# Weight chunks, a held load and a new written order in a linear-attention and FFN kernel

## The chip, the core and the metric

The kernel runs on one core of a Trainium2 chip. The core has a matrix engine (TensorE, PE in the profile), three engines for elementwise work (VectorE or DVE, ScalarE or ACT, GpSimd or POOL), and SyncE (SP), which here only issues DMAs. Each engine has its own instruction queue and works through it in order; between engines, semaphores make one wait for another. Matrix products read SBUF, the on-chip memory, and write PSUM, a small accumulator memory divided into banks. Data moves between the chip's main memory and SBUF by 16 DMA engines that all queues share.

The metric is the device time of one execution in microseconds (us).

## What is computed

Two stages run one after the other. The first is a causal linear attention with decay over 4 batches, 8 heads, 768 positions and a head size of 64; each head has its own decay `lam`. The second is an FFN on the 3072 resulting rows of 512, with a sine in its activation:

```python
intra = np.einsum('bhic,bhjc->bhij', qb, kb) * Dmask[None]
intra = np.einsum('bhij,bhjd->bhid', intra, vb)
inter = np.einsum('bhid,bhde->bhie', qb * lam_pow[None], kv_state)
out[:, :, sl] = intra + inter
kv_state = lam_block * kv_state + np.einsum('bhsd,bhse->bhde', kb_dec, vb)
# then, with x the attention's rows
h = x @ w_in                      # 512 -> 2048
s = np.sin(alpha * h)
g = h + s * s / (alpha + 1e-09)
return g @ w_out                  # 2048 -> 512
```

Inputs and output are float32; the kernel works in bfloat16 and accumulates in float32.

## The kernel before

The work is cut into six groups of 512 rows, and each group's attention into four units, numbered u = 0 to 23 (group u // 4). A unit is 256 positions of one batch and four heads.

A unit takes these steps. Three loads on SP's queue bring q, k and v in float32, 256 KB each (`ld.u.0`, `ld.u.1`, `ld.u.2`; line 256, tiles st_q, st_k, st_v, eight buffers of each). `sq`, `sk` (line 297) multiply q and k by powers of the decay and give bfloat16 tiles QL and KD; `cv` casts v. QL and KD are transposed into QT: units 0 to 7 do that on TensorE (`tq`, `tk`, line 324, then the copies `tcq`, `tck` out of PSUM), units 8 to 23 by DMA transposes on SP's queue (`tdq`, `tdk`, line 342). `s` makes scores (line 365), `m` masks them on VectorE (line 375), `k` makes the unit's state (line 401), `kc` copies it, `a` and `n` decay and accumulate it (lines 427, 431, 439). `oi` and `o` (lines 452, 466) make the output, and `x` copies it into xt, the FFN's input.

For each group g, FFN1 has 16 steps `f1.g.f` of four 128x128 by 512 products (line 489), one for each 128 columns of w_in. The first four are cut in two halves (`f1a.g.f`, then `f1.g.f`), so that the first half can start when the group's units 0 and 1 are done. `sin` (line 509), `sqr` (line 516 or 518) and `stt` (line 523) make the activation into gall. FFN2 has steps `f2.g.m.j` (line 532): 128 rows m, and a quarter j of the 2048 columns, of four products each. Step j needs activations 4j to 4j+3 and the w_out chunk j. `oc` copies the result, `st` stores it on SP's queue. The last 128 rows are done in two halves (`lt`, `ltc`, lines 555 and 565), whose last store ScalarE issues.

The weights come by DMAs that GpSimd issues and that cast float32 to bfloat16: `wi` for w_in (line 266), here five DMAs of 2, 2, 4, 4 and 4 times 128 columns (256 KB or 512 KB in SBUF), and `wo` for w_out (line 273), four of 512 KB, chunk j for FFN2's quarter j. The first of them waits until `loads[GATE]` has landed, v of unit 2. Everything behind it in GpSimd's queue waits with it.

Nothing is scheduled by a program at run time or at build time: the string ORDER lists every step with its engine (T, V, A, G, S for TensorE, VectorE, ScalarE, GpSimd, SyncE) and, for products, the PSUM bank. Reading it from start to end gives each engine's queue. `ld.4.0`, the first load of group 1 (the second group), has a wait added by hand: it is issued only after the FFN1 step named in HOLD, and all that SP issues later stands behind it. `w.n` puts n products of zeros into TensorE's queue (line 595), which nothing reads; 28 more run at the start (line 569).

Of the kernel before, what the change touches and what calls it, by code (L numbers as in the profile page):

```python
# [18 lines left out]
ld.0.0:S tab:V ld.0.1:S ld.0.2:S cv.0:A sq.0:V sk.0:G w.4:T:s1 tq.0:T:5 tcq.0:V w.5:T:s1 tk.0:T:5  # L19
tck.0:V k.0:T:0,1 a.0.0:V ld.1.0:S w.3:T:s0 s.0:T sq.1:G oi.0:T tq.1:T:2 kc.0.0:A kc.0.1:A tcq.1:A  # L20
n.0.0:G ld.1.1:S sk.1:V m.0.0:V ld.1.2:S cv.1:G tk.1:T:1 tck.1:A w.4:T:h0 k.1:T:0,2 m.0.1:V o.0:T
kc.1.0:A kc.1.1:A x.0.0:A s.1:T a.1.0:V m.1.0:V ld.2.0:S ld.2.1:S ld.2.2:S sq.2:G sk.2:G tq.2:T:1
w.3:T:okv oi.1:T tk.2:T:2 m.1.1:V o.1:T tcq.2:A cv.2:A tck.2:A x.1.0:A k.2:T:0,1 ld.3.0:S ld.3.1:S
ld.3.2:S sq.3:V sk.3:V wi.0:G wi.1:G wi.2:G cv.3:G kc.2.0:A x.1.1:A s.2:T m.2.0:V w.2:T:h3 tq.3:T:3
m.2.1:V tcq.3:A kc.2.1:A a.2.0:V tk.3:T:2 tck.3:A w.6:T:h3 k.3:T:3,1 wi.3:G n.1.0:G a.3.0:V s.3:T
oi.2:T o.2:T m.3.0:V x.2.0:A x.2.1:A kc.3.0:A m.3.1:V kc.3.1:V f1a.0.0:T:2 f1a.0.1:T:0 ap:T al:V
oi.3:T o.3:T f1a.0.2:T:1 f1a.0.3:T:3 x.3.0:V x.3.1:A f1.0.0:T f1.0.1:T sin.0.0:A sin.0.1:A sqr.0.0:V
sqr.0.1:V stt.0.0:V wi.4:G wo.0:G a.1.1:G n.2.0:G n.1.1:G f1.0.2:T f1.0.3:T f1.0.4:T:5 f1.0.5:T:4
sin.0.2:A stt.0.1:V sin.0.3:A sin.0.4:A sqr.0.2:G sqr.0.3:A w.3:T:h0 f1.0.6:T:0 sin.0.5:A sin.0.6:A
stt.0.2:V stt.0.3:V f1.0.7:T:2 sqr.0.4:G sqr.0.5:A sqr.0.6:A a.2.1:G stt.0.4:V n.3.0:G wo.1:G  # L30
sin.0.7:A stt.0.5:V sqr.0.7:V stt.0.6:V stt.0.7:V f1.0.8:T:3 f1.0.9:T:5 sin.0.8:A sqr.0.8:G
f1.0.10:T:4 sin.0.9:A sqr.0.9:V sin.0.10:A sqr.0.10:G ld.4.0:S ld.4.1:S ld.4.2:S ld.5.0:S ld.5.1:S
ld.5.2:S ld.6.0:S ld.6.1:S ld.6.2:S ld.7.0:S ld.7.1:S ld.7.2:S ld.8.0:S f1.0.11:T:1 stt.0.8:V
stt.0.9:V sin.0.11:A wo.2:G sq.4:G wo.3:G cv.4:G sqr.0.11:V stt.0.10:V sk.4:G stt.0.11:V f1.0.12:T:0
w.3:T:h3 f1.0.13:T:3 sin.0.12:A sin.0.13:A sqr.0.12:A sqr.0.13:V stt.0.12:V stt.0.13:V f1.0.14:T:2
sq.5:G a.3.1:G a.0.1:G n.0.1:G sk.5:G cv.5:G n.3.1:G sq.6:G sk.6:G cv.6:G sq.7:G sk.7:G f1.0.15:T:4
sin.0.14:A sin.0.15:A sqr.0.14:A sqr.0.15:A stt.0.14:V stt.0.15:V f2.0.1.0:T:1 f2.0.1.1:T
f2.0.0.0:T:3 tq.4:T:2 f2.0.0.1:T tcq.4:A k.4:T:4,5 kc.4.0:A kc.4.1:A a.4.0:V tk.4:T:2 tck.4:A
f2.0.2.0:T:0 oi.4:T tq.5:T:2 s.4:T f2.0.2.1:T m.4.0:V m.4.1:V tcq.5:A f2.0.0.2:T f2.0.2.2:T tk.5:T:2
f2.0.1.2:T tck.5:V s.5:T f2.0.0.3:T m.5.0:V oc.0.0:A f2.0.1.3:T oc.0.1:V o.4:T x.4.0:A k.5:T:2,3  # L40
kc.5.0:A a.5.0:V m.5.1:V kc.5.1:A f2.0.2.3:T tq.6:T:1 oi.5:T tk.6:T:2 o.5:T oc.0.2:A k.6:T:3,0
tck.6:V kc.6.0:V tcq.6:A n.4.0:G cv.7:G s.6:T m.6.0:V f2.0.3.0:T:1 m.6.1:V tq.7:T:2 tcq.7:A ld.8.1:S
# [84 lines left out]
def kernel(  # L127
# [14 lines left out]
    B, H, S, D = q.shape  # L142
# [10 lines left out]
    GATE = (2, 2)  # L153
    HOLD = (0, 9)
# [478 lines left out]
```

## Time and profile before

Seven runs took 222.51 to 225.04 us, with a median of 224.04. The profiled execution took 222.52 us, of which its records span 220.7 us.

| What | Value |
|---|---|
| median of 7 runs | 224.04 us |
| profiled execution | 222.52 us |
| its span | 220.7 us |
| TensorE's granted clock in it, mean | 0.996 |
| first product of FFN1 (`f1a.0.0`) | 18.36 us |
| load `ld.4.0` issued | 30.19 us |
| last product ends | 216.8 us |

The page gives busy time by engine, the chain of waits (from the last instruction back to whatever released each step), groups of instructions by line, and DMA issues. The timeline gives instructions in order of time, equal neighbours merged; a bracket at a line's end is idle time of that engine just before it, and what ended it. "PE" lines are products, "SPq" and "POOL ... DMA_DIRECT2D" lines are issues of DMAs: their time is that of the issue, not of the transfer. Where a DMA's landing is given, it is the time of its semaphore.

### The profile page before, as it was taken

How to read it: one execution, taken by the hardware profiler on the slowest of the kernel's cores; microseconds unless marked ns; L12 is line 12 of the kernel's file. 1: busy time of each engine (PE TensorE's matmuls, PEld its weight loads, DVE VectorE, ACT ScalarE, POOL GpSimd, SP SyncE). 2: the span in 40 equal slices, each digit the busy share in tenths (PEclk: the TensorE clock that was granted, in tenths of full speed). 3: DMA queues.
4: the chain of work that ended last, by engine and by line, in shares of the span. 5: the costliest groups of instructions: out<-in, count | busy, mean ns of one | idle time of the engine just before them, and what ended most of it. 6: DMA issues, size and time to landing. Idle time of an engine off the chain costs nothing.

```text
span 220.7 us, 5409 instructions
## 1 busy us (share of the span) xinstructions
PE 210.2 (95%) x2110; PEld 108.5 (49%) x2110; DVE 127.9 (58%) x218; ACT 126.4 (57%) x232; POOL 138.7 (63%) x208
## 2 busy tenths in 40 slices
PE   8789799999999999899999999999999999999992
PEld 6557344556755534345545444445444444444462
DVE  3694779348599988328477655357564537333020
ACT  3283696335599999254676489425873755544101
POOL 6597476869989889999969758586260703031000
PEclk9999999999999999999999999999999999999998
DMA  5999999999996899999796993325205202020824
GB/s 137 297 189 148 206 161 258 237 298 292 215 184 160 221 197 267 286 212 217 144 242 167 262 137 72 74 71 146 48 0 119 50 1 48 0 50 0 180 61 93
DMA packets 64377, 33.92 MB, mean 154 GB/s; under 512 B 19664, under 2 KB 61408, under 8 KB 64352
## 3 DMA queue, kind: packets, MB, share of 16 engines
q1 hardware_dynamic: 59488, 29.31, 58.4%
q0 software_dynamic: 4752, 4.19, 12.4%
q8 instruction: 16, 0.26, 0.5%
q10 hardware_dynamic: 112, 0.07, 0.1%
q14 instruction: 9, 0.07, 0.1%
HBM read 27.28 MB, written 6.29 MB: 152 GB/s over the span
## 4 chain that ended last, share of the span: by engine, by line
PE 73%; DMA 12%; POOL 10%; issue 1%; DVE 1%; SPq 0%; ACT 0%; POOLq 0%; ACTq 0%
PE ops L532 36%; PE hps L489 27%; DMA w_in_sb<-in_moe_w_in_dram 4%; PE okv L466 2%; DMA QT<-KD 2%; PE sp L365 2%; DMA st_k<-in_k_dram 2%; DMA st_v<-in_v_dram 2%; PE ops L555 2%; POOL s L518 1%; PE okv L452 1%; POOL kvbd L431 1%; POOL KD L297 1%; POOL QL L297 1%; DMA lam_bc<-in_lam_dram 1%
## 5 line engine op out<-in xcount | busy, mean ns | idle before, releaser
L489 PE MATMUL hps<-xt,w_in_sb 128*128 128x512 bf16 (+1 forms) x416 | 91.5, 363 | 1.8 <-DMA w_in_sb<-in_moe_w_in_dram 1.4
L523 DVE SCALAR_TENSOR_TENSOR gall<-s,r_sb,hps 128x512 bf16<-128x512 bf16 x96 | 68.6, 744 | 36.6 <-ACT s L516 22.6
L532 PE MATMUL ops<-w_out_sb,gall 128*128 128x512 bf16 x368 | 86.6, 379 | 0.0
L509 ACT ACTIVATE s<-hps,alpha_sb 128x512 bf16<-128x512 f32 x96 | 63.9, 685 | 37.2 <-PE hps L489 35.2
L518 POOL TENSOR_TENSOR s<-s 128x512 bf16<-128x512 bf16 x30 | 31.1, 1042 | 47.9 <-ACT s L509 46.3
L489 PEld LDWEIGHTS <-w_in_sb 128*128 128x128 bf16 x416 | 38.4, 98 | 40.5 <-DMA w_in_sb<-in_moe_w_in_dram 1.7
L532 PEld LDWEIGHTS <-gall 128*128 128x128 bf16 x368 | 34.3, 98 | 38.5
L516 ACT ACTIVATE s<-s 128x512 bf16<-128x512 bf16 x58 | 35.3, 627 | 1.3 <-DVE gall L523 0.5
L375 DVE TENSOR_TENSOR ST<-sp,mask 128x512 bf16<-128x512 f32 x48 | 31.8, 684 | 5.9 <-PE sp L365 5.7
L279 ACT COPY ob<-ops 128x512 f32<-128x512 f32 (+1 forms) x15 | 8.3, 555 | 30.6 <-PE ops L532 18.3
L297 POOL TENSOR_TENSOR QL<-st_q,E 128x512 bf16<-128x512 f32 x22 | 22.9, 1043 | 3.1 <-DMA st_q<-in_q_dram 2.9
L297 POOL TENSOR_TENSOR KD<-st_k,R 128x512 bf16<-128x512 f32 x22 | 23.0, 1044 | 1.9 <-DMA st_k<-in_k_dram 1.1
L431 POOL TENSOR_TENSOR kvbd<-kvx,LBD 128x256 bf16<-128x256 f32 x32 | 19.6, 614 | 2.5
L281 DVE COPY ob<-ops 128x512 f32<-128x512 f32 x10 | 6.9, 688 | 17.2 <-PE ops L532 17.2
L427 POOL TENSOR_TENSOR kvx<-kva,kvs 128x128 f32<-128x128 f32 x32 | 14.8, 462 | 1.6 <-DVE kva L281 1.6
L279 ACT CAST xt<-okv 128x512 bf16<-128x512 f32 (+1 forms) x17 | 8.8, 525 | 5.2 <-PE okv L466 3.8
L281 POOL CAST VB<-st_v 128x512 bf16<-128x512 f32 x15 | 9.2, 613 | 3.3 <-DMA st_v<-in_v_dram 3.3
L281 DVE CAST xt<-okv 128x512 bf16<-128x512 f32 (+1 forms) x10 | 6.6, 664 | 7.9 <-PE okv L466 7.7
L365 PE MATMUL sp<-QT 64*64 64x128 bf16 x384 | 9.9, 220 | 1.3 <-DMA QT<-KD 1.1
L466 PE MATMUL okv<-ST,VB 64*64 64x128 bf16 x384 | 10.2, 221 | 0.0
L439 POOL TENSOR_TENSOR kvs<-kvx,LHP 128x128 f32<-128x128 f32 x24 | 9.5, 401 | 0.0
L365 PEld LDWEIGHTS <-QT 64*64 64x64 bf16 x384 | 6.6, 106 | 5.0 <-issue 1.7
(60 smaller groups left out, 120.3 us busy)
## 6 DMA issues: line engine op xcount, KB each, us to landing
st_q<-in_q_dram SPq DMA_DIRECT2D x24, 256.0 KB, 4.7
st_k<-in_k_dram SPq DMA_DIRECT2D x24, 256.0 KB, 4.6
st_v<-in_v_dram SPq DMA_DIRECT2D x24, 256.0 KB, 4.8
out_dram<-ob SPq DMA_DIRECT2D x46, 128.0 KB, 2.5
w_out_sb<-in_moe_w_out_dram POOLq DMA_DIRECT2D x4, 512.0 KB, 8.7
w_in_sb<-in_moe_w_in_dram POOLq DMA_DIRECT2D x3, 512.0 KB, 10.7
w_in_sb<-in_moe_w_in_dram POOLq DMA_DIRECT2D x2, 256.0 KB, 4.7
QT<-QL SPq DMA_TRANSPOSE x16, 3.7
```

What stands on the lines that cost most here:

```text
L279: nc.scalar.copy(out=out, in_=in_)
L281: eng.tensor_copy(out=out, in_=in_)
L297: eng.tensor_tensor(out=t[:], in0=stage[u, j][:].rearrange("p h two e -> p two h e"), in1=tab[:, :, hh * HH:(hh + 1) * HH].unsqueeze(3).to ...
L365: nc.tensor.matmul(out=sp[hd][half[c], par, hp, :], lhsT=QT[half[hd], 1, par, hp, half[c]], rhs=QT[half[hd], 0, :, hp, half[c]], start=Tru ...
L375: nc.vector.tensor_tensor(out=stm[u][:, hd], in0=sps[u][hd][:], in1=mask[:].unsqueeze(2).to_broadcast([P, 2, 2, P]), op=ALU.mult)
L431: eng.tensor_tensor(out=kvbd[u, c][:], in0=x.unsqueeze(2).to_broadcast([P, 2, 2, D]), in1=LBD[:, 2 * hh:2 * hh + 2, :].unsqueeze(3).to_bro ...
L489: f1mm[g, f] = nc.tensor.matmul(out=hps[g, f][:].rearrange("p (b i) -> p b i", b=2)[:, bs] .rearrange("p b i -> p (b i)"), lhsT=w_in_sb[:, ...
L509: nc.scalar.activation(out=s1[g, f][:], in_=hps[g, f][:], func=ACTF.Sin, scale=alpha_sb[:, f:f + 1])
L516: nc.scalar.activation(out=s2[g, f][:], in_=x[:], func=ACTF.Square)
L518: eng.tensor_tensor(out=s2[g, f][:], in0=x[:], in1=x[:], op=ALU.mult)
L523: nc.vector.scalar_tensor_tensor(out=gall[g][:, f, :], in0=s2.pop((g, f))[:], scalar=r_sb[:, f:f + 1], in1=hps.pop((g, f))[:], op0=ALU.mul ...
L532: nc.tensor.matmul(out=ops[g, m][:], lhsT=gall[g][:, f, m * P:(m + 1) * P], rhs=w_out_sb[:, f, :], start=(f == 0), stop=(f == NFC - 1))
```

## The change

Three constants change. w_in comes in four DMAs of 4 x 128 columns instead of five. The first of these waits for k of unit 2 instead of v of unit 2. `ld.4.0` waits for FFN1 step 14 of group 0 instead of step 9. The string ORDER is replaced as a whole. It has the same steps with these differences in number: one `wi` less; 20 instead of 33 warm-up products between the steps; some copies, casts, scalings and squares on another engine (ScalarE has 10 steps more, VectorE 9 fewer, GpSimd 2 fewer). No function changes. The lists below are cut to the first stage and the end; in both the middle is left out.

```diff
--- before.py
+++ after.py
@@ -16,111 +16,111 @@
 ORDER = """
-ld.0.0:S tab:V ld.0.1:S ld.0.2:S cv.0:A sq.0:V sk.0:G w.4:T:s1 tq.0:T:5 tcq.0:V w.5:T:s1 tk.0:T:5
...
-ld.3.2:S sq.3:V sk.3:V wi.0:G wi.1:G wi.2:G cv.3:G kc.2.0:A x.1.1:A s.2:T m.2.0:V w.2:T:h3 tq.3:T:3
-m.2.1:V tcq.3:A kc.2.1:A a.2.0:V tk.3:T:2 tck.3:A w.6:T:h3 k.3:T:3,1 wi.3:G n.1.0:G a.3.0:V s.3:T
...
-sqr.0.1:V stt.0.0:V wi.4:G wo.0:G a.1.1:G n.2.0:G n.1.1:G f1.0.2:T f1.0.3:T f1.0.4:T:5 f1.0.5:T:4
-sin.0.2:A stt.0.1:V sin.0.3:A sin.0.4:A sqr.0.2:G sqr.0.3:A w.3:T:h0 f1.0.6:T:0 sin.0.5:A sin.0.6:A
-stt.0.2:V stt.0.3:V f1.0.7:T:2 sqr.0.4:G sqr.0.5:A sqr.0.6:A a.2.1:G stt.0.4:V n.3.0:G wo.1:G
...
-f1.0.10:T:4 sin.0.9:A sqr.0.9:V sin.0.10:A sqr.0.10:G ld.4.0:S ld.4.1:S ld.4.2:S ld.5.0:S ld.5.1:S
-ld.5.2:S ld.6.0:S ld.6.1:S ld.6.2:S ld.7.0:S ld.7.1:S ld.7.2:S ld.8.0:S f1.0.11:T:1 stt.0.8:V
-stt.0.9:V sin.0.11:A wo.2:G sq.4:G wo.3:G cv.4:G sqr.0.11:V stt.0.10:V sk.4:G stt.0.11:V f1.0.12:T:0
-w.3:T:h3 f1.0.13:T:3 sin.0.12:A sin.0.13:A sqr.0.12:A sqr.0.13:V stt.0.12:V stt.0.13:V f1.0.14:T:2
-sq.5:G a.3.1:G a.0.1:G n.0.1:G sk.5:G cv.5:G n.3.1:G sq.6:G sk.6:G cv.6:G sq.7:G sk.7:G f1.0.15:T:4
-sin.0.14:A sin.0.15:A sqr.0.14:A sqr.0.15:A stt.0.14:V stt.0.15:V f2.0.1.0:T:1 f2.0.1.1:T
-f2.0.0.0:T:3 tq.4:T:2 f2.0.0.1:T tcq.4:A k.4:T:4,5 kc.4.0:A kc.4.1:A a.4.0:V tk.4:T:2 tck.4:A
-f2.0.2.0:T:0 oi.4:T tq.5:T:2 s.4:T f2.0.2.1:T m.4.0:V m.4.1:V tcq.5:A f2.0.0.2:T f2.0.2.2:T tk.5:T:2
-f2.0.1.2:T tck.5:V s.5:T f2.0.0.3:T m.5.0:V oc.0.0:A f2.0.1.3:T oc.0.1:V o.4:T x.4.0:A k.5:T:2,3
-kc.5.0:A a.5.0:V m.5.1:V kc.5.1:A f2.0.2.3:T tq.6:T:1 oi.5:T tk.6:T:2 o.5:T oc.0.2:A k.6:T:3,0
...
-st.4.2.0:S st.4.2.1:S f2.5.0.3:T f2.5.1.0:T:5 f2.5.1.1:T f2.5.1.2:T f2.5.1.3:T f2.5.2.0:T:3
-f2.5.2.1:T f2.5.2.2:T f2.5.2.3:T lt.0:T:2 lt.1:T:4 st.4.0.0:S st.4.0.1:S oc.5.0:A st.5.0.0:S
-st.5.0.1:S oc.5.1:V st.5.1.0:S st.5.1.1:S oc.5.2:V st.5.2.0:S st.5.2.1:S ltc.0:A ltc.1:A
+ld.0.0:S ld.0.1:S ld.0.2:S ld.1.0:S tab:V sq.0:V ld.1.1:S ld.1.2:S sk.0:G w.4:T:h2 tq.0:T:2 cv.0:A
+tk.0:T:4 k.0:T:0,1 a.0.0:V sk.1:V ld.2.0:S tcq.0:A tck.0:A w.4:T:s0 s.0:T sq.1:G kc.0.0:A oi.0:T
+tq.1:T:2 tcq.1:A ld.2.1:S ld.2.2:S ld.3.0:S ld.3.1:S wi.0:G ld.3.2:S wi.1:G tk.1:T:0 tck.1:A cv.1:A
...
+kc.2.1:A x.1.1:A w.3:T:okv oi.2:T cv.3:G o.2:T x.2.0:A x.2.1:A k.3:T:2,3 kc.3.0:A kc.3.1:A m.3.0:V
+m.3.1:V n.0.0:G wi.2:G wi.3:G wo.0:G wo.1:G a.0.1:G a.3.0:V ap:T f1a.0.0:T:1 f1a.0.1:T:5 oi.3:T
+o.3:T al:V f1a.0.2:T:0 f1a.0.3:T:4 x.3.0:V x.3.1:A f1.0.0:T sin.0.0:A sqr.0.0:V f1.0.1:T sin.0.1:A
+n.0.1:G sqr.0.1:G stt.0.0:V f1.0.2:T n.2.0:G stt.0.1:V wo.2:G a.2.1:G f1.0.3:T sin.0.2:A sin.0.3:A
...
+stt.0.5:V stt.0.6:V stt.0.7:V f1.0.8:T:5 sin.0.8:A f1.0.9:T:4 sin.0.9:A sqr.0.8:G sqr.0.9:G
+stt.0.8:V stt.0.9:V f1.0.10:T:3 sin.0.10:A sqr.0.10:A stt.0.10:V f1.0.11:T:1 f2.0.0.0:T:2
+f1.0.12:T:0 sin.0.11:A sin.0.12:A sqr.0.11:V sqr.0.12:A f1.0.13:T:5 f1.0.14:T:3 sin.0.13:A
+stt.0.11:V f2.0.0.1:T f2.0.1.0:T:1 f1.0.15:T:4 f2.0.1.1:T f2.0.1.2:T f2.0.0.2:T ld.4.0:S stt.0.12:V
+ld.4.1:S ld.4.2:S ld.5.0:S ld.5.1:S ld.5.2:S ld.6.0:S ld.6.1:S ld.6.2:S ld.7.0:S ld.7.1:S ld.7.2:S
+ld.8.0:S ld.8.1:S ld.8.2:S sin.0.14:A sqr.0.13:A ld.9.0:S ld.9.1:S ld.9.2:S stt.0.13:V wo.3:G
+n.3.0:G a.3.1:G n.3.1:G sin.0.15:A f2.0.2.0:T:0 n.1.0:G a.1.1:G sqr.0.14:G n.1.1:G stt.0.14:V
+sqr.0.15:G sq.4:G sk.4:G stt.0.15:V f2.0.0.3:T sq.5:G sk.5:G oc.0.0:A cv.4:A sq.6:G sk.6:G
+f2.0.2.1:T f2.0.1.3:T tq.4:T:5 tk.4:T:3 f2.0.2.2:T tcq.4:V tck.4:V s.4:T k.4:T:2,3 kc.4.0:A kc.4.1:A
+cv.5:A oc.0.1:V m.4.0:V a.4.0:V f2.0.2.3:T tq.5:T:4 tk.5:T:3 oi.4:T k.5:T:1,2 m.4.1:V oc.0.2:A o.4:T
+cv.6:G tcq.5:A kc.5.0:A tck.5:V s.5:T tq.6:T:0 n.4.0:G x.4.0:A sq.7:G sk.7:G kc.5.1:V a.5.0:V
+tk.6:T:3 f2.0.3.0:T:2 m.5.0:V m.5.1:V tcq.6:A oi.5:T a.4.1:G sq.8:G sk.8:G tck.6:A ld.10.0:S
+ld.10.1:S ld.10.2:S k.6:T:1,0 kc.6.0:A kc.6.1:A cv.7:A o.5:T a.6.0:V x.5.0:A s.6:T m.6.0:V m.6.1:V
...
+f2.5.1.1:T f2.5.1.2:T f2.5.1.3:T f2.5.2.0:T:2 f2.5.2.1:T f2.5.2.2:T oc.5.0:A st.5.0.0:S st.5.0.1:S
+oc.5.1:A st.5.1.0:S st.5.1.1:S f2.5.2.3:T lt.0:T:0 oc.5.2:A ltc.0:A lt.1:T:1 st.5.2.0:S ltc.1:A
+st.5.2.1:S
 """
...
@@ -150,8 +150,8 @@
     NFC = DFF // P
     NU = 4 * NG
     RING = 8
-    GATE = (2, 2)
-    HOLD = (0, 9)
+    GATE = (2, 1)
+    HOLD = (0, 14)
     XSPLIT = (1, 2, 3)
     N0 = 28
     assert NDC == HP
@@ -233,7 +233,7 @@
     w_out_sb = wpool.tile([P, NFC, DM], BF16, name="w_out_sb")
 
     WCH = 4
-    W_IN = (2, 2, 4, 4, 4)
+    W_IN = (4, 4, 4, 4)
     BANK = ("h0", "h1", "h2", "h3", "s0", "s1")
 
     def psum(shape, dtype, name, bank):

```

In the new order `wi.0` and `wi.1` stand behind `sq.1` in GpSimd's queue, `wi.2`, `wi.3`, `wo.0` and `wo.1` follow `n.0.0`, `wo.2` follows `n.2.0`, and `wo.3` follows `sqr.0.9`. On TensorE ten steps of FFN2 of group 0 stand ahead of `tq.4`, where there were three.

## The prediction

> **What bounds the kernel now.** I read the page's busy row first, then the chain of waits, then the timeline of TensorE for every place where it waits.
>
> ```profile
> PE 210.2 (95%) x2110; PEld 108.5 (49%) x2110; DVE 127.9 (58%) x218; ACT 126.4 (57%) x232; POOL 138.7 (63%) x208
> PE 73%; DMA 12%; POOL 10%; issue 1%; DVE 1%; SPq 0%; ACT 0%; POOLq 0%; ACTq 0%
> 14.87 9.35 DMA w_in_sb<-in_moe_w_in_dram
> 24.27 1.90 PE hps L489 x8
> 26.55 6.20 PE hps L489 x28
> 32.79 0.50 PE bz L595 x3
> 33.34 2.75 PE hps L489 x12
> ```
>
> TensorE is busy in 210 of 220.7 us, so the end is set by when it starts real work and by what it waits for after that. The chain shows the start: the third w_in DMA, issued at 14.87, lands at 24.22 and releases the FFN1 step f1.0.4 at 24.27. From there the chain is almost all TensorE. The timeline gives its waits in brackets:
>
> ```profile
> 24.27 1.90 PE L489 MATMUL hps<-xt,w_in_sb 128*128 128x512 bf16 x8 [1.41 <-DMA w_in_sb<-in_moe_w_in_dram]
> 81.66 1.02 PE L489 MATMUL hps<-xt,w_in_sb 128*128 128x512 bf16 x4 [0.32 <-DVE gall L523]
> 89.75 0.42 PE L365 MATMUL sp<-QT 64*64 64x128 bf16 x16 [1.08 <-DMA QT<-KD]
> ```
>
> These are the only bracketed waits from 18.4 us on: 1.41 + 0.32 + 1.08 = 2.81 us. The rest is matmuls, so the change can win from three things only: those waits, TensorE work that is not needed, and an earlier start.
>
> **TensorE work.** The products are the same in both orders. Two things differ. After f1a.0.0 the old order has two warm-up groups of three (26.00 and 32.79; 0.55 us each until the next product), the new one has one: **-0.55**. The other ten fewer warm-ups lie before f1a.0.0, where TensorE waits anyway: nothing. Then the alternation between the 64-row attention products (k, s, o) and all others:
>
> ```profile
> 38.73 1.03 PE L532 MATMUL ops<-w_out_sb,gall 128*128 128x512 bf16 x4
> 39.69 0.32 PE L401 MATMUL kvp<-VB,KD 64*64 64x64 bf16 x16
> ...
> 53.17 0.42 PE L365 MATMUL sp<-QT 64*64 64x128 bf16 x16
> 53.42 0.29 PE L401 MATMUL kvp<-VB,KD 64*64 64x64 bf16 x16
> ```
>
> Start to start, four FFN2 matmuls take 0.96 us ahead of a 64-row block (38.73 to 39.69), but 0.86 ahead of a 128-row one (40.18 to 41.04). A block of scores takes 0.25 us ahead of another 64-row block (53.17 to 53.42), but 0.35 ahead of FFN2 (45.60 to 45.95). So going down and back costs 0.20 us. Counted in the order after f1a.0.0, the old list goes down 42 times, the new 38: 4 x 0.20 = **-0.80**.
>
> **The front: w_in.** The two old 256 KB chunks land at 17.15 and 19.57, 2.42 apart; the last 512 KB chunks at 26.82 and 29.34, 2.5 apart. A small chunk costs the queue as much as a large one (the trace has 512 packets for either), so four instead of five frees some 2.4 us. The gate moves from st_v to st_k of unit 2 (landings 12.44 and 11.54), and wi.0 stands behind sq.1 on POOL (done 9.09) instead of sk.2 (done 13.22): the issue moves from 13.17 to about 11.6. POOL waits there for the gate, with wi.1, sq.3, cv.2 and cv.3 behind it; unit 3's q lands only at 13.34, so the POOL work behind loses nothing.
>
> When data flows is not certain. In the old trace wi.0's first packet comes 1.6 us after its issue; wo.2's comes 3.7 us after (32.93 to 36.6), while loads filled the engines. So flow starts between 13.2 and 15.3. Here a rule speaks against the change. The Trainium skill, DMA: Bandwidth & Descriptors, "Queues, rings and completion order", says that each DMA engine takes turns between queues, packet by packet. The row nearest to that is st_k landing beside w_out: 5.8/9.5/11.0 us (minimum, median, maximum) in 30 to 42 us, against 4.1/5.4/5.7 alone at the start. By the rule, from 13.2 on the remaining two loads (about 660 packets, ending at 14.4 alone) would end near 18; unit 3's mask work on VectorE would come late and f1a.0.0 move from 18.3 to 19.9. By the 3.7 us row nothing collides, and only the early gate is wasted. Between the two I take the flow from about 14.5.
>
> Now FFN1. Following the new order by the durations of the old rows (mask 0.64 twice per unit, scale 0.69 on VectorE or 1.04 on POOL, copies 0.59 on ScalarE), with the loads landing as before: the second mask of unit 1 ends at 13.9, unit 2's at 16.35, s.3 comes at 16.4, oi.2 at 17.25, k.3 at 17.9, and f1a.0.0 at **18.3**, as before (18.36). Chunk 0 needs 2.4 us (row of the first chunk) to 4.65 us (19.57 to 24.22, the third) of flow: landed between 15.6 and 19.9. Chunk 1, which now holds f1.0.4, comes 2.6 later: 18.2 to 22.5. So the 1.41 us wait before f1.0.4 goes, if chunk 0 is there by 18.3; if it lands at 19.9, the wait has only moved ahead of f1a.0.0. Gain 0 to 1.41, and -0.2 by the collision; I take **-0.90**.
>
> A second rule speaks against it: TensorE: Matmul & The Clock Gate, Part 1, says that after an idle window of about 3.4 us the clock halves. PEclk is 1.00 across the old wait of 1.41 us. The longest new wait I find is 1.6 us (chunk 0 at 19.9). By the row this costs nothing; by the rule a wait beyond 3.4 us would make the next 3.4 us half as fast, +1.7. I take the row.
>
> **The hold.** SP's queue stops at ld.4.0 until f1.0.14 instead of f1.0.9; behind it stand every later load, all DMA transposes and all stores. With f1.0.4 near 23.4 and 0.863 us per FFN1 or FFN2 step (four matmuls), f1.0.14 is done near 34.3, against 30.19 before. The work that hides this: f2 steps are moved ahead of unit 4's transposes, ten instead of three, so TensorE reaches tq.4 near 42.9. The loads then run alone, where before they shared the engines:
>
> ```profile
> 28.55 0.79 POOL L273 DMA_DIRECT2D w_out_sb<-in_moe_w_out_dram  x1
> 32.93 0.80 POOL L273 DMA_DIRECT2D w_out_sb<-in_moe_w_out_dram  x1
> 36.66 0.79 POOL L273 DMA_DIRECT2D w_out_sb<-in_moe_w_out_dram  x1
> 36.44 2.39 SPq L256 DMA_DIRECT2D st_k<-in_k_dram  x1
> 38.87 3.25 SPq L256 DMA_DIRECT2D st_v<-in_v_dram  x1
> 42.16 1.25 SPq L256 DMA_DIRECT2D st_q<-in_q_dram  x1
> ```
>
> At 36 to 44 us one load issue takes 1.3 to 3.3 us, because w_out is in the engines. In the new order wo.0 and wo.1 are issued right behind wi.3 (near 18), wo.2 behind sqr.0.1 (near 24), wo.3 behind sqr.0.9 (near 30.5). At 2.5 us a chunk the queue ends with wo.3 near 36 to 38. f2.0.0.3, the first user, comes near 40.3: 2 us to spare. ld.4.0 lands near 38.5, then 0.9 us each: unit 7 near 48.5, against 49.2 to 51.4 before. POOL scales unit 4 after sqr.0.15 (38.8): ready at 40.8, 2 us ahead of tq.4. After tq.4 only 6 f2 steps are left as filler, where the old order had 13. VectorE has there 8 masks (5.1), 4 kvbd (1.7), 4 copies of transposes (1.7) and one each of kva, ob and xt (1.6), 10.1 us within TensorE's 12. Followed unit by unit it is never more than 0.3 us late. I count the hold at 0.
>
> **What was late next.** The waits at 81.66 and 89.75 came from VectorE and from SP's queue (a transpose issued at 84.83, landing 4.87 us later). SP should reach ld.10.0 some 3 us earlier. Adding up the orders by the rows' durations from f1a.0.0 on, POOL has 42 us of work ahead of sk.13 instead of 47, TensorE 69 ahead of s.13 instead of 66. So both waits should go: **-1.40**. But ScalarE gets 4 us more work and no order meets its own plan exactly: I put half of that back, **+0.70**.
>
> **The end.** st.5.2.1 now stands behind the last piece's DMA on SP. Before, the last copy is followed by a DMA of 2.22 us (issued by ScalarE). Now 0.51 us of SP's issue come first, then about 2.3 us: 0.51 + 2.3 - 2.2 = **+0.64**, rounded up.
>
> **Sum**: -0.55 - 0.80 - 0.90 - 1.40 + 0.70 + 0.64 = -2.3 us. The profiled execution took 222.52 (220.7 and 1.8 around it), so 220.2; the runs' median is 224.04, 1.5 above it, so 224.04 - 2.3 = **221.7**.
>
> **Rivals.** (a) *No change*, 223.7 (chance 0.18): the collision eats the front (-0.90 becomes +0.2), and the two later waits are replaced by equal ones (+0.70). -2.3 + 1.1 + 0.7 = -0.5. For it: ScalarE and POOL are busy 5.3 of 5.5 us between 60 and 72. Against: POOL and SP run ahead.
> (b) *Slower*, 225.4 (0.28): the last w_out chunk becomes the wait. f2.0.0.3 used to start at 45.95, just after wo.3 had landed at 45.71, 9.05 us after its issue; now TensorE stands at it near 40.3 with unit 4 queued behind. At 44.0 it waits 3.7: -2.3 + 3.7 = +1.4. It costs the whole gain from a landing at 42.6, and decides for slower from 43.7. For it: wo.2 took 3.7 us to start and 8.44 to land beside loads. Against: it is issued 6 us earlier, ahead of the loads.
> (c) *Nothing hidden is exposed and w_in comes early*: all of 1.41 and nothing put back, -3.5, 220.5. This is the forecast's lower part.
> Forecast with (c): 0.54.
>
> About 0.5% (1.1 us) can be told from no change. Faster 0.54, same 0.18, slower 0.28. The range goes from 219.5 (-3.5 and 1 us for how runs scatter) to 226.0, which takes in (a) and (b); the forecast's own is 219.5 to 222.9.
>
> **What would show it.** f1.0.4 starts near 23.4 with no wait above 0.5; no wait for w_out at f2.0.0.3; tq.4 near 43; no bracket above 0.5 at s.12 to s.16; four fewer descents on TensorE; the last store issued by SP after the last copy. Wrong if f1a.0.0 starts after 19.9, if wo.3 lands after 42, or if new brackets past 60 us add up to more than 2 us.

## The result and the profile after

Twelve runs of the changed kernel have a median of 221.16 us (219.55 to 224.77); the kernel before, on the same chip, took 223.75 us. The ratio is 0.9874, with an interval of 0.9841 to 0.9906: faster by 2.1 to 3.6 us. Ratios and intervals here are of the fast runs alone (those at most 1.5% above the fastest of the same kernel), so they are not the quotients of the medians. On two more chips the unaltered changed kernel gave 221.52 us (0.9917, 0.9887 to 0.9946) and 221.28 us (0.9912, 0.9878 to 0.9946). By the medians the gain is 1.9 to 2.6 us; the prediction was 2.3 (224.0 to 221.7).

Three profiles of the changed kernel exist, and they differ: their runs took 224.77, 222.39 and 219.92 us. The first one is of the longest of its twelve runs. Its busy row, its granted clock in 40 slices, and its chain of waits by engine:

```profile
PE 210.4 (94%) x2097; PEld 109.2 (49%) x2097; DVE 123.5 (55%) x209; ACT 130.5 (59%) x242; POOL 139.1 (62%) x206
PEclk9999999999999999969999999999999999999999
PE 71%; POOL 9%; DMA 8%; SPq 4%; issue 3%; ACT 2%; DVE 1%; POOLq 0%; ACTq 0%
```

TensorE is still the bound, but one slice of the clock row, the 18th, is a 6. The timeline of TensorE, first at the start of FFN1 and then at that slice:

```profile
17.89 0.49 PE L595 MATMUL bz<-zeros 128*128 128x256 bf16 x3 [0.83 <-ACT xt L279]
...
19.27 1.05 PE L489 MATMUL hps<-xt,w_in_sb 128*128 128x256 bf16 x8
...
21.00 4.30 PE L489 MATMUL hps<-xt,w_in_sb 128*128 128x256 bf16 x31
...
93.83 0.42 PE L466 MATMUL okv<-ST,VB 64*64 64x128 bf16 x16
96.03 0.42 PE L365 MATMUL sp<-QT 64*64 64x128 bf16 x16 [1.78 <-DMA QT<-KD]
96.38 3.25 PE L489 MATMUL hps<-xt,w_in_sb 128*128 128x512 bf16 x8
```

The wait of 1.41 us for w_in is gone: from 21.00 on, FFN1 runs through f1.0.4 (at 23.63) without a bracket. f1a.0.0 itself comes at 19.27, 0.9 later than before, held by ScalarE's copy of xt. The two later waits of before are gone too, but a new one of 1.78 us stands at 96.03, at s.14, for its DMA transpose (`tdk.14`, the transpose of k for unit 14); two smaller ones, of 0.36 and 0.18, stand at 73.19 and 77.58. After s.14, eight products of FFN1 take 3.25 us; at full speed they take 1.9 (24.27 in the profile before). The granted clock and the busy time of the engines in three neighbouring stretches of 3.41 us show why:

```profile
93.35:96.76 3.41, 1.63 (x37) 0.78 (x36) 0.27 (x1) 1.33 (x3) 3.25 (x8) 1.00 0.95 146
96.76:100.17 3.41, 3.41 (x10) 1.22 (x8) 3.02 (x5) 1.81 (x3) 3.33 (x6) 0.50 0.54 114
100.18:103.59 3.41, 3.41 (x46) 1.61 (x45) 1.39 (x3) 1.18 (x3) 1.54 (x3) 1.00 0.58 134
```

The columns are the stretch, its length, the busy time of PE, PEld, DVE, ACT and POOL, then the granted clock, the DMA share and GB/s. In the first stretch TensorE is busy for 1.63 us; in the next its clock is 0.50; then it is 1.00 again. So this run lost 1.78 us by the wait and some 1.7 by the clock.

The second profile waits 0.60 us at 67.07 and 1.15 at s.14, and its clock stays full. The third, the control on the last chip, has no such wait: span 218.1 us, and no bracket above 0.16 us from 18 us on. In the table, f1a.0.0 and f1.0.4 are steps of FFN1, f2.0.0.3 the first step that needs the last w_out chunk, tq.4 the first transpose of group 1.

| start of | before | after, first | second | third |
|---|---|---|---|---|
| f1a.0.0 | 18.36 | 19.27 | 19.00 | 18.84 |
| f1.0.4 | 24.27 | 23.63 | 23.36 | 23.20 |
| f2.0.0.3 | 45.95 | 40.75 | 40.48 | 40.33 |
| tq.4 | 38.51 | 43.34 | 43.07 | 42.91 |
| s.14 (its place in the order differs) | 99.02 | 96.03 | 95.34 | 92.85 |
| wait at s.14 | none | 1.78 | 1.15 | none |
| end of the last product | 216.81 | 218.12 | 215.75 | 213.23 |
| span | 220.74 | 222.99 | 220.61 | 218.10 |
| span less the last product's end | 3.93 | 4.87 | 4.87 | 4.87 |

### The profile page after: what moved, and what is told of

Read it like the earlier page. It is cut to its first block, busy times and chain, and to the rows that moved or that the text cites. A ratio compares the mean times of both kernels' runs of the same rounds, so it can differ in the third digit from the quotient of the medians.

```text
span 223.0 us, 5364 instructions
## 1 busy us (share of the span) xinstructions
PE 210.4 (94%) x2097; PEld 109.2 (49%) x2097; DVE 123.5 (55%) x209; ACT 130.5 (59%) x242; POOL 139.1 (62%) x206
## 4 chain that ended last, share of the span: by engine, by line
PE 71%; POOL 9%; DMA 8%; SPq 4%; issue 3%; ACT 2%; DVE 1%; POOLq 0%; ACTq 0%
PE ops L532 33%; PE hps L489 28%; DMA st_k<-in_k_dram 3%; DMA QT<-KD 3%; SPq L256 2%; PE okv L466 2%; POOL QL L297 2%; DMA st_v<-in_v_dram 2%; PE sp L365 2%; POOL KD L297 2%; PE ops L555 2%; PE okv L452 1%; POOL kvbd L431 1%; POOL kvs L439 1%; SPq L342 1%
## 5 line engine op out<-in xcount | busy, mean ns | idle before, releaser
L518 POOL TENSOR_TENSOR s<-s 128x512 bf16<-128x512 bf16 x34 | 35.1, 1043 | 43.8 <-ACT s L509 38.5
L489 PEld LDWEIGHTS <-w_in_sb 128*128 128x128 bf16 x416 | 39.1, 98 | 40.3 <-issue 2.4
L516 ACT ACTIVATE s<-s 128x512 bf16<-128x512 bf16 x54 | 33.3, 630 | 0.7
L297 POOL TENSOR_TENSOR KD<-st_k,R 128x512 bf16<-128x512 f32 x21 | 21.8, 1044 | 2.6 <-PE sp L365 2.0
L279 ACT COPY ob<-ops 128x512 f32<-128x512 f32 (+1 forms) x16 | 8.9, 558 | 23.1 <-PE ops L532 17.6
L279 ACT CAST xt<-okv 128x512 bf16<-128x512 f32 (+1 forms) x21 | 11.4, 546 | 10.3 <-PE okv L466 8.8
L427 POOL TENSOR_TENSOR kvx<-kva,kvs 128x128 f32<-128x128 f32 x32 | 14.7, 458 | 3.7 <-ACT kva L279 1.9
L279 ACT CAST VB<-st_v 128x512 bf16<-128x512 f32 x13 | 8.1, 619 | 3.5 <-DMA st_v<-in_v_dram 3.5
L452 PEld LDWEIGHTS <-kvbd 128*128 128x128 bf16 x80 | 6.1, 98 | 5.1 <-DVE kvbd L431 0.6
L452 PE MATMUL okv<-QT,kvbd 128*128 128x128 bf16 x80 | 8.4, 219 | 0.2
```

Of the source, the lines that this page charges most:

```text
L279: nc.scalar.copy(out=out, in_=in_)
L297: eng.tensor_tensor(out=t[:], in0=stage[u, j][:].rearrange("p h two e -> p two h e"), in1=tab[:, :, hh * HH:(hh + 1) * HH].unsqueeze(3).to ...
L452: nc.tensor.matmul(out=okv[u][:, c, hp * P:(hp + 1) * P], lhsT=sts[c][:, hp].rearrange("p two e -> p (two e)"), rhs=QT[:, 0, :, hp, half[c ...
L489: f1mm[g, f] = nc.tensor.matmul(out=hps[g, f][:].rearrange("p (b i) -> p b i", b=2)[:, bs] .rearrange("p b i -> p (b i)"), lhsT=w_in_sb[:, ...
L516: nc.scalar.activation(out=s2[g, f][:], in_=x[:], func=ACTF.Square)
L518: eng.tensor_tensor(out=s2[g, f][:], in0=x[:], in1=x[:], op=ALU.mult)
```

## The experiments

Each kernel ran against the kernel before on the same chip (median 223.4, 223.9 and 223.46 us on the three).

| kernel | median, us | ratio to before (interval) |
|---|---|---|
| **first chip** | | |
| after_again: the changed kernel | 221.52 | 0.9917 (0.9887 to 0.9946) |
| tail_swap | 220.73 | 0.9882 (0.9844 to 0.9919) |
| hold9 | 220.40 | 0.9888 (0.9844 to 0.9931) |
| five_chunks | 221.89 | 0.9923 (0.9892 to 0.9955) |
| **second chip** | | |
| before_4chunks | 222.81 | 0.9947 (0.9914 to 0.9980) |
| sp14 | 222.58 | 0.9947 (0.9907 to 0.9987) |
| order_only | 223.29 | 0.9974 (0.9934 to 1.0014) |
| warm6 | 224.44 | 1.0034 (0.9995 to 1.0074) |
| **third chip** | | |
| after_third: the changed kernel | 221.28 | 0.9912 (0.9878 to 0.9946) |
| tail_hold11 | 220.60 | 0.9869 (0.9827 to 0.9910) |
| order_warm | 221.22 | 0.9914 (0.9877 to 0.9950) |
| descents8 | 223.68 | 0.9993 (0.9960 to 1.0027) |

### The controls

> The changed kernel once more, for a profile to set the others beside. Theory A (the sum of the prediction): the span of an execution without the 1.78 us wait at 94.25 and the half clock behind it (3.41 us at half, 1.7 us) is 223.0 - 1.8 - 1.7 = 219.5 us; f1.0.4 starts at 23.6, f1a.0.0 at 19.3, the last product ends 4.9 us before the span does. Ratio to the kernel before 0.984 to 0.991. Rival theory B (the changed order is bound by the DMA transposes behind SP's queue, the lost 3.5 us belong to it): a wait of 1 us or more for QT at s.12 to s.16 comes again, and the span stays above 221.

> The changed kernel once more, unaltered, as the control of this chip. All theories: ratio to the kernel before 0.985 to 0.992, about 221 us. For the scatter at s.14: if SP's queue sets it (transposes tdq.14 and tdk.14 behind loads and stores), this profile shows a wait for the DMA QT<-KD near 94 us of some size between 0 and 1.8 us, with tdk.14 landing between 93.8 and 96; a wait anywhere else of over 0.5 us would speak against it.

Beside the medians above, these give the scatter. tdk.14 was issued at 90.17, 90.38 and 88.91 us in the three profiles and took 5.81, 4.92 and 3.54 us to land. Over the eleven profiles of the new order with tdk.14 in its place, TensorE waits at s.14 where that DMA took 4.9 us or more, and does not where it took 3.4 to 3.8. (A profile is of one run: with these waits, the three spans above differ by 4.9 us.)

### The price of a warm-up group (warm6)

Six groups of three products of zeros are added in the last group's FFN1, where TensorE is always busy:

```diff
-f1.5.3:T:5
+w.3:T:s1 f1.5.3:T:5
```

and so ahead of f1.5.4, f1.5.6, f1.5.11, f1.5.12 and f1.5.13, each in the bank of its successor.

> The changed kernel with six more groups of three warm-up products in the FFN1 steps of the last group, where TensorE is always busy. Theory A (each group costs what the forecast took, 0.55 us, or 0.75 with the drain of the product ahead of it): 3.3 to 4.5 us more than after_again, 1.5 to 2.0%. Rival theory B (they fall into hidden waits): less than 1 us.

In TensorE's timeline of this kernel, a group and what follows it:

```profile
175.18 0.49 PE L595 MATMUL bz<-zeros 128*128 128x256 bf16 x3
175.73 1.02 PE L489 MATMUL hps<-xt,w_in_sb 128*128 128x512 bf16 x4
```

From f1.5.0 to f1.5.15 it takes 29.16 us instead of 25.90: 3.26 for six groups, **0.54 each**. The prediction's 0.55 stands.

### The price of a descent (descents8)

A descent is a change from a 128-row product to a 64-row one on TensorE. Here eight are added:

```diff
-s.12:T k.12:T f1.2.4:T:3
+s.12:T f1.2.4:T:3 k.12:T
```

and likewise k.15, k.21, k.22, k.23 one FFN step away from the scores ahead of them, s.16, s.17 and s.19 one step away from the attention block ahead of them.

> The changed kernel with eight attention products taken out of their neighbourhood: k.12, k.15, k.21, k.22, k.23 each stand one FFN step behind the scores they followed, and s.16, s.17, s.19 one step behind the o or k block they followed. TensorE goes from 128-row to 64-row products 46 times after f1a.0.0 instead of 38; the products are the same. By the prediction's 0.20 us for down and back: 8 x 0.20 = +1.6 us on the changed kernel of the same chip, from s.12 to s.23 (about 87 to 155 us). If the 0.20 belongs only to where a wait or a pipelined end is read (a modelled end), the time stays within 0.3 us.

TensorE's timeline round s.12, in the control and in this kernel:

```profile
80.64 0.42 PE L365 MATMUL sp<-QT 64*64 64x128 bf16 x16
80.89 0.29 PE L401 MATMUL okv<-VB,KD 64*64 64x64 bf16 x16
81.18 2.75 PE L489 MATMUL hps<-xt,w_in_sb 128*128 128x512 bf16 x11
```

```profile
81.84 0.42 PE L365 MATMUL sp<-QT 64*64 64x128 bf16 x16
82.38 1.02 PE L489 MATMUL hps<-xt,w_in_sb 128*128 128x512 bf16 x4
83.33 0.32 PE L401 MATMUL okv<-VB,KD 64*64 64x64 bf16 x16
83.58 1.90 PE L489 MATMUL hps<-xt,w_in_sb 128*128 128x512 bf16 x7
...
101.31 0.38 PE L452 MATMUL okv<-QT,kvbd 128*128 128x128 bf16 x4 [0.54 <-ACT kva L279]
```

The same products: from s.12 to s.13 it is 8.72 us instead of 8.36. Over four stretches (s.12 to s.13; s.14 to f1.3.8 without the bracket of 0.54; f1.3.8 to s.20; s.20 to f1.5.0) the eight moves cost 0.36 + 0.51 + 0.56 + 0.68 = 2.11 us, **0.26 each** rather than 0.20. The bracket is a second price: f2.1.2.3 had hidden ScalarE's copy of k.15's state, and once it stands ahead of k.15 the next product waits for that copy. The medians differ by 2.40 us.

### w_in alone (before_4chunks, five_chunks)

The first is the old kernel with four equal chunks, the second the changed kernel with the five old ones:

```diff
-    W_IN = (2, 2, 4, 4, 4)
+    W_IN = (4, 4, 4, 4)
-wi.0:G wi.1:G wi.2:G
+wi.0:G wi.1:G
```

> The kernel before with w_in in four equal chunks, nothing else changed. Theory A (the forecast's front term: two half chunks cost the queue nearly as much as two whole ones): the columns of f1.0.4 land near 20.5 to 21.5 instead of 24.22, the wait of 1.41 us there goes, and chunk 0 lands near 18.5, at most 0.3 us after TensorE wants it (18.36): 0.4 to 0.6% faster than the kernel before. Rival theory B (the wait only moves): chunk 0 lands near 19.5 to 20 and TensorE waits 1 us or more at f1a.0.0; within 0.2% of the kernel before.

> The changed kernel with w_in in the old five chunks. Theory A (two half chunks cost the queue as much as two whole ones, 2.4 us each): columns for f1.0.4 land 2 to 4 us later than 20.6, near 23 to 24.5, and f1.0.4 (23.6) waits 0 to 0.9 us; 0.2 to 0.5% slower than after_again. Rival theory B (the chunks are hidden behind the attention of the first group): f1.0.4 does not wait, within 0.2%.

In the old order, TensorE's timeline with four chunks reads:

```profile
19.23 1.05 PE L489 MATMUL hps<-xt,w_in_sb 128*128 128x256 bf16 x8 [0.31 <-DMA w_in_sb<-in_moe_w_in_dram]
...
20.94 4.52 PE L489 MATMUL hps<-xt,w_in_sb 128*128 128x256 bf16 x31
```

The first chunk lands at 19.18, TensorE waits 0.31 us for it at f1a.0.0, and the 1.41 us at f1.0.4 are gone: f1.0.4 stands at 23.57, 0.70 earlier, and the ratio is 0.5% below 1. In the new order five chunks make no difference to the median that can be told (0.9923 against 0.9917). But its profile shows what the fifth chunk costs there. GpSimd issues three w_in DMAs instead of two ahead of its scaling of q for unit 3, and tq.3 waits for that:

```profile
15.60 0.61 PE L324 MATMUL pt<-iden,QL 128*128 128x128 bf16 x4 [0.91 <-POOL QL L297]
```

A half-clock stretch follows, and f1.0.4 stands at 24.82, 1.2 to 1.6 later than in the three profiles of the changed kernel; its columns of w_in had landed at 22.18, so f1.0.4 does not wait for them. In the second and the first of these chunk 0 lands at 18.10 and 18.11 whether it is issued at 11.55 or 12.21, some 3 us after the last of the first twelve loads (14.7 and 15.2).

### The order alone, and the clock (order_only, order_warm)

order_only is the new order with the three old constants: five chunks, the gate on v of unit 2, the hold at f1.0.9.

> The changed kernel's order with all three constants as before: five chunks, the gate on v of unit 2, the hold on FFN1 step 9. Theory A (the order alone carries the gain, the constants next to nothing): ratio to the kernel before 0.985 to 0.992, within 0.3% of after_again, f1.0.4 without a wait above 0.5 us, and 0.6 us of wait at f2.0.0.3 as with the hold alone undone. Rival theory B (the constants carry it): f1.0.4 waits 1 us or more and the ratio is above 0.995.

It loses most of the gain: its interval reaches 1. TensorE's timeline and its stretches:

```profile
16.51 0.40 PE L324 MATMUL pt<-iden,QL 128*128 128x128 bf16 x4 [1.80 <-POOL QL L297]
...
21.42 1.89 PE L489 MATMUL hps<-xt,w_in_sb 128*128 128x256 bf16 x8
```

```profile
14.50:17.90 3.40, 1.60 (x45) 1.07 (x45) 1.94 (x4) 1.29 (x4) 3.39 (x7) 1.00 1.12 130
17.95:24.70 6.75, 6.13 (x85) 4.16 (x85) 2.93 (x8) 1.86 (x9) 4.37 (x7) 0.50 1.18 177
24.80:28.20 3.40, 3.35 (x27) 2.53 (x26) 1.17 (x2) 2.51 (x6) 1.00 (x1) 1.00 1.24 206
```

GpSimd scales q of unit 3 only behind the gate and three w_in issues (12.93 to 15.39); tq.3 waits 1.80 us for it. Then TensorE runs at half clock for 6.8 us: the first eight FFN1 products take 1.89 instead of 1.05. In 10 of its 12 runs the mean granted clock was 0.971 to 0.985. To tell the wait from the clock, the next kernel fills the wait:

```diff
-oi.1:T tq.3:T:2
+oi.1:T w.10:T:h2 tq.3:T:2
```

> The order-only kernel (new order, five chunks, gate on v of unit 2, load held by FFN1 step 9; 223.29 us, ratio 0.9974) plus ten products of zeros on TensorE just ahead of tq.3, where it waited 1.80 us and then ran 6.8 us at half clock. If the clock gate is what makes that kernel slow there, the ten products (about 1.1 us) fill the wait, the half-clock stretch near 18 us goes, and f1.0.4 moves from 26.86 to about 24.5 us: -2 us, ratio about 0.988. If the late scaling of unit 3's q on POOL is the whole cost and the clock only follows, f1.0.4 stays within 0.5 us of 26.9 and the ratio at 0.997.

```profile
15.16 1.25 PE L595 MATMUL bz<-zeros 128*128 128x256 bf16 x10 [0.18 <-ACT kva L279]
16.47 0.38 PE L324 MATMUL pt<-iden,QL 128*128 128x128 bf16 x4
...
20.59 1.05 PE L489 MATMUL hps<-xt,w_in_sb 128*128 128x256 bf16 x8
```

```profile
14.50:17.90 3.40, 3.15 (x69) 2.18 (x57) 2.23 (x5) 1.45 (x4) 3.39 (x6) 1.00 1.28 153
17.95:24.70 6.75, 5.76 (x103) 4.53 (x103) 3.01 (x9) 2.94 (x11) 4.10 (x7) 1.00 1.14 176
```

tq.3 starts at the same time (16.47 against 16.51), so the data come no earlier; but TensorE was busy for 3.15 of 3.40 us instead of 1.60, the clock stays at 1.00, and f1.0.4 moves from 26.97 to 24.95. The ratio goes from 0.9974 to 0.9914: ten products that compute nothing gain some 0.6%, or 1.3 us, and 2.0 us at f1.0.4. The two ratios are of two chips and their intervals just overlap; the clock is the firmer sign, since no run of order_warm has a mean clock below 0.994.

### The hold (hold9)

```diff
-    HOLD = (0, 14)
+    HOLD = (0, 9)
```

> The changed kernel with ld.4.0 held until FFN1 step 9 again. Theory A (the hold only keeps the loads away from w_out): ld.4.0 goes out near 29.5 instead of 34.9, the last w_out chunk lands 3 to 6 us later than 39.5[...], and TensorE waits at f2.0.0.3 (at 40.75 now) for it by 2 to 4 us; 1 to 2% slower than after_again. Rival theory B (the hold is idle): w_out lands in time, less than 0.5 us of new waits, within 0.3% of after_again. Rival theory C (the hold costs): the group two attention comes earlier and the span shrinks by 0.5 us or more.

In TensorE's timeline, f2.0.0.3 now waits for the last chunk of w_out:

```profile
41.43 2.75 PE L532 MATMUL ops<-w_out_sb,gall 128*128 128x512 bf16 x12 [0.63 <-DMA w_out_sb<-in_moe_w_out_dram]
```

That chunk, issued at 31.89, landed at 41.39; with the hold at f1.0.14 it took 31.59 to 37.61 in the control. But there SP comes to its later work sooner (tdk.14 issued at 88.0 instead of 88.9 to 90.4, landed at 91.4), s.14 does not wait in this profile, and the median is no worse.

### SP's queue (sp14)

```diff
-tdk.13:S
+tdk.13:S tdq.14:S tdk.14:S st.0.1.0:S ld.16.1:S ld.16.2:S ld.17.0:S
```

(with these six taken out of their old places behind).

> The changed kernel with unit 14's two DMA transposes issued right behind tdk.13, ahead of one store and the loads 16.1, 16.2 and 17.0 in SP's queue. Theory A (what is left of TensorE's waits, 0 to 1.8 us at s.14, is SP's queue being late with tdk.14, landing 93.8 to 96.0): tdk.14 lands by 92, s.14 waits nothing, 0.4 to 0.6% faster than after_again (ratio to the kernel before 0.985 to 0.988), last product at 214.6 or earlier. Rival theory B (the stall moves to the loads that were passed): a new wait of 0.5 us or more at unit 16 or 17, no gain. Rival theory C (the transfer itself takes up to 5.8 us wherever it stands): the wait at s.14 comes in spite of it.

tdk.14 lands at 89.2 and s.14 no longer waits, but the timelines of VectorE and of TensorE have two new brackets:

```profile
96.06 0.69 DVE L281 COPY ob<-ops 128x512 f32<-128x512 f32 x1 [1.43 <-DMA out_dram<-ob]
96.81 0.38 PE L532 MATMUL ops<-w_out_sb,gall 128*128 128x512 bf16 x1 [1.07 <-DVE ob L281]
```

The copy is that of f2.1.1 (`oc.1.1`), into the ob buffer that the stores st.0.1.0 and st.0.1.1 read. The store that was moved, st.0.1.0, has landed at 90.13. It is st.0.1.1, left in its place, that holds the buffer: issued at 90.70, it lands only at 96.04 (90.15 and 93.97 in the third profile of the changed kernel). VectorE's copy waits 1.43 us for it, and FFN2 1.07 us for the PSUM bank behind the copy. One wait has taken the other's place; why that store took 5.3 us to land, no run shows.

### The end (tail_swap, tail_hold11)

```diff
-st.5.2.0:S ltc.1:A st.5.2.1:S
+st.5.2.0:S st.5.2.1:S ltc.1:A
```

> The changed kernel with st.5.2.1 issued ahead of the last copy's DMA. Theory A: the end behind the last product shrinks from 4.9 us by 0.5 to 0.9 to about that of the kernel before (3.9), so 0.3% below after_again. Rival theory B: the end is set by something that follows the last landing in either order; the tail stays within 0.2 us of 4.9.

The stretch behind the last product goes only from 4.87 to 4.57 us, since SP's issue for the last piece stands behind one store more. The second version puts both stores ahead of the last block's first half, and sets the hold to f1.0.11:

```diff
-oc.5.2:A ltc.0:A lt.1:T:1 st.5.2.0:S ltc.1:A st.5.2.1:S
+oc.5.2:A st.5.2.0:S st.5.2.1:S ltc.0:A lt.1:T:1 ltc.1:A
-    HOLD = (0, 14)
+    HOLD = (0, 11)
```

> The changed kernel with the two stores of the row block before last (st.5.2.0, st.5.2.1) issued right behind their copy, ahead of both stores of the last block's first half, and with the held load after FFN1 step 11 instead of 14. If the tail is the chain of SP's issues (five of 0.51 to 0.63 us behind the first half's copy), it shrinks from 4.87 us after the last product to about 3.8, -1.0; exchanging only the last two gave -0.3. The hold: with step 9 TensorE waited 0.63 us for the last chunk of w_out, with step 14 not at all; with 11 a wait of 0 to 0.3 is expected, and SP about 1.2 us earlier at tdk.14 than with 14, so the wait at s.14 near 0. Together 1.0 to 2.0 us below the changed kernel on the same chip: ratio to before 0.978 to 0.985. If the tail is set by the transfer time of the last store alone, or by the copies, only 0 to -0.3.

SP's queue at the end, of the control and of this kernel:

```profile
211.92 1.11 SPq L565 DMA_DIRECT2D out_dram<-ob  x2
213.07 0.59 SPq L547 DMA_DIRECT2D out_dram<-ob  x1
213.76 0.54 SPq L565 DMA_DIRECT2D out_dram<-ob  x1
214.35 0.84 SPq L547 DMA_DIRECT2D out_dram<-ob  x1
```

```profile
210.45 4.04 SPq L547 DMA_DIRECT2D out_dram<-ob  x3
214.87 2.26 SPq L565 DMA_DIRECT2D out_dram<-ob  x3
```

In the control the last issue is a full store (line 547) behind the last piece (line 565); here the pieces are last. The stretch behind the last product is 3.93 us, as in the kernel before: the tail is mended, -0.94. The hold was not: f2.0.0.3 waits

```profile
41.88 2.32 PE L532 MATMUL ops<-w_out_sb,gall 128*128 128x512 bf16 x10 [1.02 <-DMA w_out_sb<-in_moe_w_out_dram]
```

and s.14 another 1.11 us. The ratio of 0.9869 is the lowest of all kernels run, but its interval overlaps that of the control (0.9912). The mended end with the hold left at f1.0.14 was not tried.

## Why the prediction was right, step by step

**Warm-up group, -0.55**: right; 0.54 measured.

**Four fewer descents, -0.80**: right in mechanism; at 0.26 each in descents8 it would be -1.05. Together with the warm-up group that makes -1.6, where the prediction had -1.35. Read directly, the gain is smaller: the work from f1.0.4 to the last product, without waits above 0.16 us and without the lost clock, is 191.1 us before, and 190.5, 190.5 and 190.0 in the three profiles of the changed kernel (189.7 in hold9), so -0.7 to -1.4. What takes part of it back stays open.

**The front, -0.90**: right in size (f1.0.4 0.64, 0.91 and 1.07 earlier in the three profiles), and before_4chunks shows that in the old order four chunks alone give 0.70 of it. The path was another than described: f1a.0.0 comes at 18.84 to 19.27 instead of 18.3, because the attention ahead of it waits for ScalarE's copy of xt (the bracket of 0.83), and w_in, landed at 18.1, is hidden behind that. Of the collision of w_in with the loads little came: the slowest of the first loads took 6.25 us instead of 5.8, and the last ones had landed by 14.7 to 15.2 (14.9 before). The first packets of w_in moved at 13.1 to 13.9, when at most 325 of the loads' 6480 packets were left, so the collision that the first rule prices hardly took place.

**The clock rule, dismissed by the row**: here the prediction was wrong. It took from the old wait of 1.41 us at PEclk 1.00 that a wait of 1.6 us costs nothing, and from the rule that only one beyond 3.4 us would. order_only against order_warm shows a wait of 1.80 us behind which the clock alone costs 2.0 us, and the first profile shows the same behind 1.78 us at s.14. What counts is not the length of one gap; the last section shows what the traces say instead. That the sum held is because the changed kernel's own front keeps clear of this: in the third profile tq.3 starts at 14.67 with a wait of 0.18. The gate and the number of chunks both have a part in that, since both let GpSimd scale q of unit 3 earlier: with five chunks tq.3 waits 0.91 us, and with five chunks and the gate on v of unit 2, 1.80 (one profile each). That worth of the two was not in the prediction.

**The hold, 0**: right at its place. The last chunk of w_out landed at 37.6 to 39.5, f2.0.0.3 stands at 40.3 to 40.8 without a wait, and tq.4 at 42.9 to 43.3 (42.9 predicted). Rival (b), a landing at 42.6 or later, is refuted. With the loads released earlier (hold9, tail_hold11) the landing is at 41.4 to 41.8 and the wait 0.63 to 1.02, so the hold removes a wait; but hold9 is not slower. In its profile SP's earlier transposes spare the wait at s.14; that this is what pays for it in the median is not shown. SP did not reach ld.10.0 three us earlier, as the prediction said, but 1.1 to 1.8 (50.4 to 51.1 against 52.2).

**Later waits, -1.40, with +0.70 put back**: the two old waits are gone, and what came back is mostly at s.14: 0, 1.15 and 1.78 us in three profiles. By the prediction's own signs this part is not clean: "no bracket above 0.5 at s.12 to s.16" fails in two profiles of three, and the brackets past 60 us of the first add up to 2.32 us, above the 2 us that it named as wrong. From the start of s.14 to the end of the last product it is 120.4 us in every profile with the new order unaltered there and the clock at 1.00. So the end is set by when s.14 starts: when TensorE gets there or, if that is later, when tdk.14 lands. That would also explain why a better front shows so little: order_warm reaches f1.0.4 1.75 us later than the third profile, but without a wait it starts s.14 at 94.39, between the 92.85 and 96.03 of the changed kernel, and the medians are the same. With one profile of it this is argued, not shown. Why the DMA takes 3.4 us in one run and 5.8 in another stays open; no run isolates it.

**The end, +0.64**: right in mechanism, too small: +0.94, and -0.94 when undone. In the control the last copy ends at 213.68; SP gets to the last store 0.67 us later, not 0.51, and that store lands 2.62 us after its issue, not 2.3. (The prediction's three numbers add up to 0.6, not 0.64. Another slip of its sums: rival (a) at -0.5 is 223.5, not 223.7.)

The terms, read from each profile against the profile before, close its span:

| term | predicted | first | second | third |
|---|---|---|---|---|
| front: start of f1.0.4 | -0.90 | -0.64 | -0.91 | -1.07 |
| work from there to the last product | -1.35 | -0.68 | -0.67 | -1.11 |
| waits above 0.16 us there | -0.70 | +0.92 | +0.52 | -1.40 |
| half clock there | 0 | +1.71 | 0 | 0 |
| the end | +0.64 | +0.94 | +0.94 | +0.94 |
| sum | -2.31 | +2.25 | -0.12 | -2.64 |
| span | | +2.24 | -0.13 | -2.64 |

So the mechanisms are right, but that the medians moved by so nearly 2.3 us is in part luck. The waits and the clock alone spread the three profiles over 4 us, the work gained less than forecast and the end cost more, and the profile before was itself of a run 1.5 us below the median of its seven.

## What to carry to other kernels

Price a mode switch and a filler group from the start-to-start times of a profile: tests that multiplied them gave 0.54 and 0.26 us for 0.55 and 0.20 here. Before products without use are taken out of a stretch with waits, count the products that are left in 3.4 us there, and not only the longest gap. And relieving one wait can make another: when a store, transpose or load is moved, follow what stands behind it in the queue to whoever waits for its buffer.

## What the hardware showed that was not expected

Half-clock stretches came in multiples of 3.41 us, each behind 3.4 us in which TensorE was busy for 1.60, 1.63 and 2.23 us; the last is five_chunks, where the longest single wait was 0.91 us:

```profile
12.10:15.50 3.40, 2.23 (x45) 1.34 (x45) 3.40 (x7) 2.07 (x5) 3.39 (x5) 0.99 1.16 210
15.50:18.90 3.40, 3.21 (x59) 2.29 (x60) 1.49 (x4) 1.66 (x5) 3.40 (x7) 0.50 1.16 146
```

In warm6 a wait of 1.70 us at s.14 did not halve the clock:

```profile
92.83:96.24 3.41, 1.55 (x33) 0.86 (x24) 1.09 (x2) 0.71 (x3) 3.33 (x7) 1.00 0.64 110
96.24:99.65 3.41, 3.41 (x28) 1.46 (x29) 2.86 (x5) 2.40 (x4) 3.33 (x6) 1.00 0.55 117
```

The Trainium skill, TensorE: Matmul & The Clock Gate, Part 1, "What's actually happening", says that the gate watches a free-running window of 3413 ns. These traces agree: in the clock record of each, every stretch between two changes lasts a whole number of 3.413 us (in order_only 13.653 at full clock, 6.827 at half, 197.973 at full), so the changes give the grid of windows. The warm6 stretch above is one such window, and the whole wait lies in it. So it is not enough to say where in a window a gap falls, and busy time does not decide either: 1.55 us stayed at full clock, 2.23 us in five_chunks did not.

What separates them is the work done. Count the products that start in a window: one of 128x512 on the whole array as 1, every other by its columns and by the part of the array that it uses (a 64x64 one with 128 columns is 1/16). A full window holds 15.8, at 0.216 us each. The fourteen traces have 876 windows at full clock that another follows. All with less than 5.5 were followed by half clock (order_only 5.25, the first profile 5.0), all with 6.0 or more by full clock (warm6 6.0); of the five with 5.5, four went to half (five_chunks among them) and one stayed. This is a count made afterwards, in traces that lack some records, and most of the low windows lie at a kernel's end. Fillers as in order_warm lift a window far above the bound; no run varies the work near it to test it.
